# One raw buffer for the wb tiles, a transposition kept off the row turn, and score banks one step sooner, in a fused attention and MLP kernel

## The chip, the cores and the metric

The kernel runs on one core of one Trainium2 chip. The metric is the device time of one execution in microseconds. The core has a matrix engine (TensorE, PE in the profile; its weight loads are listed apart as PEld), a vector engine (VectorE, DVE), a scalar engine (ScalarE, ACT), a general engine (GpSimd, POOL) and a queue that issues the transfers (SyncE, SP). Each of them runs its own instructions in the order in which the program lists them.

## The reference

```python
x = A_x                                    # 1 x 2048 x 512
xn = layernorm(x)
q = (xn @ wq)                              # 32 heads of 16
k, v = xn @ wk, xn @ wv                    # one head of 16, shared by all
p = softmax(einsum("bhqd,bkd->bhqk", q, k) * 16 ** -0.5)
s = einsum("bhqk,bkd->bhqd", p, v) @ wo    # 512 x 512
h = xn @ w1 + b1                           # 512 x 1792
act = h * tanh(softplus(h))                # Mish
g = silu(act @ w2)                         # 1792 x 512
out = x + s * g
```

All arrays are float32.

## The kernel before, in words

**Tiling.** The 2048 rows are handled in four chunks `c` of 512 columns of the transposed, normalised input `xt`. A chunk has eight *units* of four heads, so there are 32 units `v`. The scores of a unit take 16 *steps*, one for each block of 128 keys, so there are 512 steps `s` (`NS`), with `v, k = divmod(s, 16)`.

**What a step does** (loop at L1257). Four score matmuls `e` (`e_one`, L871), each of 128 keys by 512 queries, are turned by ACT into `pt = exp(e / 4)` (L873). Four matmuls `m` (`m_one`, L890) compute scores of a later unit the other way round, 128 queries by 512 keys, and DVE takes the maximum of each row (L892). They run `LEAD = 22` steps ahead, so the last 22 steps, from step `NS - LEAD = 490`, have none. At the end of the step come the `pv` matmuls of step `s - 2` (L938). `e` uses one half of the rows of the PE array and `m` the other, and the two run at once. Between them `waves` places filler: matmuls of the projections, cut into halves of the array (`xps`, L106), up to eight to a step. A filler *group* of 12 or 15 matmuls is begun by `begin` when `is_ready` says that its weights and inputs are there by the planner's reckoning; otherwise the step has no filler. The matmuls of a group stand in the PE order, so if its weights come later than reckoned, PE waits in the middle of the step.

**The row turn** (`c_rows`, L898). When the 64 maxima columns of a unit are done, DVE reduces them (`mx`), and two steps later PE transposes the result (`mt`, L911, in a bank of tag `m`), DVE splits it in a high and a low part (`cr`), and SP copies both into rows 48, 49, 112 and 113 of the unit's query tile `qt` (L925, four transfers). The score matmuls of the unit subtract the maxima in this way.

**Weights.** A tile of `w1` has tag `ws`, one of `w2` or `wo` tag `wb`, one of `wq` tag `wq`. On its first use a tile is loaded as float32 into a *raw* buffer (`load`, L418 or L420); there are `RAWS = 2` of these for all tags together, and `NRAW` says how many of them a tag may hold at a time. POOL then splits it into a high part (L145) and a low part (L150), and the raw buffer is free. The split tile is also stored to DRAM (L399), and from its second use on it is loaded from there (L412). `pump` goes through the tags in the order wq, ws, wb, wx at the end of each step. POOL also does most of Mish, the scaling of the attention output (`oc`, `ot_all`) and the splits of `q`.

**SP's queue** carries all of this in order: raw loads, stores of split tiles, the query rows of coming units (L583), the maxima rows (L925) and the rows of the output (L956). An instruction whose buffer is not free yet holds up what is behind it.

**The transposed input of chunks 2 and 3** (`xt_turns`). Four tiles each are transposed by PE (L812, in a bank of tag `m`) at the end of odd steps, copied by ACT (L815) and split by POOL. In the kernel before, those of chunk 2 stand in steps 181, 183, 185 and 187, those of chunk 3 in steps 323 to 329.

**Banks.** PSUM tag `e` has three buffers, tag `m` three, tag `v` (pv) one and tag `x` (filler) one.

**Before step 0** a planner written into the kernel (L1166 on) lists layer norm, transposition of the input, the projections of k, v and the first q, 44 pairs of `m` matmuls, single matmuls that keep PE busy (`keep_warm`, L1152) and the first filler groups, by estimated costs. It loads and splits weights with the same `load` and `split`. k is computed for one chunk of keys at a time (`kp`, L277) and copied to the second half of the rows by a transfer (L288); pairs 24 to 31 of unit 0 need the k of chunk 3.

By the listed order of the kernel before, steps 4, 41, 86, 87, 136, 157, 158 and 479 have no filler.

Of the kernel before, what the change touches and what calls it, by code (L numbers as in the profile page):

```python
# [33 lines left out]
LEAD = 22  # L34
# [23 lines left out]
def m_need(v):  # L58

    return (40, 64)[v] if v < 2 else 32 * (v + 1)  # L60
# [52 lines left out]
def block_kernel(ctx: ExitStack, tc: tile.TileContext, x, wq, wk, wv, wo, w1, b1, w2, out):  # L113
# [3 lines left out]
    ps_e = ctx.enter_context(tc.tile_pool(name="ps_e", bufs=3, space=bass.MemoryType.PSUM))  # L117
    ps_m = ctx.enter_context(tc.tile_pool(name="ps_m", bufs=3, space=bass.MemoryType.PSUM))
# [195 lines left out]
    def at(s, fn):  # L314
        if s <= step[0]:
            fn()
        else:
            timed.setdefault(s, []).append(fn)

    def later(k, fn):  # L320
        at(step[0] + k, fn)
# [22 lines left out]
            ran[0] += 1  # L344

    RING = {"wq": 1, "ws": 2, "wb": 5, "wx": 4}
    NRAW = {"wq": 1, "ws": 1, "wb": 2, "wx": 1}
    RAWS = 2
    raws = [0]
    items = {t: [] for t in RING}  # L350
# [9 lines left out]
    def arrived(tag):  # L360
        k, n = todo[tag]
        return k < n and items[tag][k].step + 1 <= (step[0] if lead else max(step[0], busy[0] / STEP_US) + 0.3)
# [39 lines left out]
    def load(tag):  # L402
# [7 lines left out]
        if n == k and kept.get(it.key):  # L410
# [3 lines left out]
            todo[tag][:] = n + 1, n + 1  # L414
        elif n - k < NRAW[tag] and raws[0] < RAWS:
            r = sb.tile([P, D], F32, tag="raw", name=f"raw{tag}{n}", bufs=RAWS)
# [8 lines left out]
    def pump():  # L425
        for tag in items:
            while arrived(tag):
                split(tag)
            load(tag)
# [63 lines left out]
    def waves(h, em, new):  # L493

        fresh = cur["g"] is None
        if not cur["chunk"] and (not new or cur["g"] is None and not begin()):
            mms = []  # L500
        else:
            g = cur["g"]
            mms = cur["chunk"] or g.mms[cur["n"]:cur["n"] + chunk_size(len(g.mms) - cur["n"])]
        second = bool(cur["chunk"])
        k = len(mms)
        ms = em(k, fresh)
        a = deque(ms[1 - h])
        b = deque(ms[h])
        ps = cur["ps"]
        ends = second and cur["n"] + k == len(cur["g"].mms)  # L510
        xs = deque(mms)
        spare = len(b) if fresh and k else 0
        relay = None
        first = True
        done = False
        while a or b or xs:
            if spare and b:
                b.popleft()()
                spare -= 1
            elif xs:  # L520
                i = xs.popleft().half(ps, h)
                if first and cur["relay"] is not None:
                    tc.add_manual_dep(i.ins, cur["relay"].ins.name, mybir.DependencyInfo(
                        mybir.DependencyClass.Sync, mybir.DependencyReason.DATA), reason="other half of the bank")
                first = False
                if not xs and ends:
                    cur["n"] += k
                    cur["chunk"] = []
                    finish()
                    done = True  # L530
            elif b:
                b.popleft()()
            if len(a) > 1 or a and not xs:
                r = a.popleft()()
                if k and not xs and relay is None:
                    relay = r
        if k and not done:
            assert relay is not None
            cur["relay"] = relay
            if second:  # L540
                cur["n"] += k
                cur["chunk"] = []
            else:
                cur["chunk"] = mms
# [235 lines left out]
    turns = deque()  # L780
# [79 lines left out]
    def e_one(s, i):  # L860

        v, r = divmod(s, 16)
        if s < NS - LEAD:
            a, k, p = 1 - s % 2, r - r % 2 + i // 2, i % 2
        else:
            a, k, p = i % 2, r, i // 2
        q = qt_of[v]
        o = 64 * a
        ps, tag = (ps_m, "m") if NS - LEAD + 1 <= s and i in ((1, 3) if s < NS - 4 else (3,)) else (ps_e, "e")
        e = ps.tile([P, C], F32, tag=tag, name=f"e{s}_{i}")  # L870
        pe.matmul(e, ks[o:o + 64, P * k:P * (k + 1)], q[o:o + 64, p], start=True, stop=True)  # L871
        pt = sb.tile([P, C], F32, tag="pt", name=f"pt{s}_{i}", bufs=NPT)
        r = act.activation(pt, e, AF.Exp, scale=0.25)  # L873
        pt_of[16 * v + k, p, a] = pt
        return r
# [3 lines left out]
    def m_one(a):  # L879
        v, n = MSEQ[m_next[a]] if m_next[a] < 64 else divmod(m_next[a], 32)  # L880
        m_next[a] += 1
        if v not in mb_of:
            mb_of[v] = sb.tile([P, 4, 16], F32, tag="mb", name=f"mb{v}", bufs=2)
        q = qt_of[v]
        kb, j = divmod(n, 8)
        p, t = divmod(j, 4)
        o = 64 * a
        m = ps_m.tile([P, C], F32, tag="m", name=f"m{v}_{a}_{n}")
        o = slice(o, o + (HALF if v < len(qts) else 48))
        pe.matmul(m, q[o, p, P * t:P * (t + 1)], ks[o, C * kb:C * (kb + 1)], start=True, stop=True)  # L890
        z = 8 * a + 4 * p + t
        return dve.reduce_max(out=mb_of[v][:, kb, z:z + 1], in_=m, axis=AX.X)  # L892

    def m_sides(h, n):

        ahead = m_next[h] - m_next[1 - h]
        lo = max((4 - MLAG - ahead + 1) // 2, 4 - (32 * NU - m_next[1 - h]))
        hi = min((4 + MLAG - ahead) // 2, 32 * NU - m_next[h])  # L898
        return max(min(n, hi), lo)
# [112 lines left out]
    NS = 16 * NU  # L1012

    nc.scalar.preload_act_table_set("natural_log_exp_and_others")
    def due(t):
        step[0] = t
        for k in sorted(k for k in timed if k <= t):
            for fn in timed.pop(k):
                fn()
# [134 lines left out]
    def m_ready(t):  # L1154
        if min(m_next) >= 2 * LEAD or rows and rows[-1].end is None:
            return None
        v, n = MSEQ[m_next[0]]
        if len(qready.get(v) or ()) <= n % 8 // 4 or n // 8 not in kready:
            return None
        return max(t, qready[v][n % 8 // 4], kready[n // 8], m_ends[-2])  # L1160
# [13 lines left out]
    while True:  # L1174
# [8 lines left out]
        m = m_ready(T["PE"])  # L1183
# [10 lines left out]
        s, e, k = min(opts, key=lambda o: o[0])  # L1194
# [36 lines left out]
        elif k == "J":  # L1231
            tag = next((g for g in ("wq", "ws", "wb") if arrived(g) and busy[0] + E0 < s + 0.5), None)
# [21 lines left out]
        k.end = now[0]  # L1254
    lead.clear()

    for s in range(NS + 2000):  # L1257
        inm = s < NS - LEAD
        if inm or cur["chunk"]:
            assert s < NS  # L1260
            due(s)
            h = s % 2

            def em(k, fresh):
                n = m_sides(1 - h, k // 2) if inm else 0
                x = deque(lambda i=i: e_one(s, i) for i in range(4))
                y = deque(lambda: m_one(1 - h) for _ in range(n))
                r = [[], []]
                for op in EM[fresh and n == 3]:
                    if op == "M" and y:  # L1270
                        r[1 - h].append(y.popleft())
                    elif op == "E":
                        r[1 - h].append(x.popleft())
                r[h] = [lambda: m_one(h) for _ in range(4 - n if inm else 0)]
                return r

            if s >= 2 and (s - 1) % 16 == 0 and s > 1:
                gap[0] += 1
            waves(h, em, inm)
            act_jobs(1 + (len(jobs) > 3))  # L1280
            due(s + 0.5)
            if s >= 2:
                pv(s - 2)
                if (s - 1) % 16 == 0 and s > 1:
                    o_out((s - 17) // 16)
                elif turns and inm and s % 2 and turns[0]():
                    turns.popleft()
        else:
            due(s)
            if s < NS:  # L1290
                for i in range(4):
                    e_one(s, i)
                fill(4)
            act_jobs(2 if s < NS else 100)
            if s < NS + 2:
                pv(s - 2)
                if (s - 1) % 16 == 0:
                    o_out((s - 17) // 16)
            due(s + 0.5)
            if s >= NS:  # L1300
                fill(16)
        step[0] = s
        if vdone[0] < 8 * NC and min(m_next) >= m_need(vdone[0]):
            r = c_rows(vdone[0])
            r[0]()
            later(2, lambda r=r: [fn() for fn in r[1:]])
            vdone[0] += 1
        pump()
        if s > NS + 1 and not queue and cur["g"] is None and not timed and not jobs:
            break  # L1310
# [12 lines left out]
```

## Time and profile before

| What | Value |
|---|---|
| median of three runs | 1647.51 us (1647.10 to 1650.88) |
| profiled execution, its own time | 1648.34 us |
| its span, first to last instruction | 1646.6 us |
| PE busy, share of the span | 1626.7 us, 99% |
| DVE busy | 1351.5 us, 82% |
| ACT busy | 1303.5 us, 79% |
| POOL busy | 638.3 us, 39% |
| mean granted PE clock | 0.997 |
| `e` of step 0 / first `pv` matmul (step 2) | 95.45 us / 102.47 us after the span's start |

Busy time is the time in which an engine has at least one instruction running. Share of the span is an average over stages: with PE at 99% a gain is to be looked for in single places where PE waits. In the listings below a line of the timeline is: start in us, duration in us, engine, line of the code, operation, tile written and tiles read, shape, count, and in brackets the idle time of the engine before it and what ended it. `SPq` is SP issuing a transfer, `DMA` a transfer on its way.

### The profile page before, as it was taken

The page shows a single profiled execution, that of the slowest core. Times are in us where ns is not written, and L with a number is a line of the kernel's source. Part 1 is how long each engine was busy: PE and PEld are TensorE (multiplying, and loading weights), DVE is VectorE, ACT ScalarE, POOL GpSimd, SP SyncE. Part 2 cuts the span into 40 slices and gives each one's busy share as a digit, 9 for nine tenths or more (in the row PEclk, how much of TensorE's full clock was granted, in tenths as well). Part 3 has the DMA queues.
Part 4 walks back from the last instruction along what each step waited for, and adds up shares of the span by engine and source line. Part 5 has one row for each costly group of instructions (what it writes and reads, how often), then busy time and mean ns, then how long its engine had stood idle before and what let it go on. Part 6 is the DMA issues. An engine that isn't in the chain of part 4 may idle for free.

```text
span 1646.6 us, 31447 instructions
## 1 busy us (share of the span) xinstructions
PE 1626.7 (99%) x11719; PEld 861.1 (52%) x11719; DVE 1351.5 (82%) x2268; ACT 1303.5 (79%) x2503; POOL 638.3 (39%) x648
## 2 busy tenths in 40 slices
PE   8999999999999999999999999999999999999998
PEld 5545545545555555555555555555555555555543
DVE  8888878888888888888888888888888888888812
ACT  5568778788888778877888787887888878788885
POOL 4764176164365202622515221271251415125421
PEclk9999999999999999999999999999999999999999
DMA  5211132142131303203122231320322213031020
GB/s 164 59 62 50 45 135 73 43 144 69 50 122 58 115 26 132 69 14 99 54 70 77 62 100 31 111 63 16 119 94 81 68 48 102 16 107 55 8 84 26
DMA packets 69640, 120.24 MB, mean 73 GB/s; under 512 B 17840, under 2 KB 31664, under 8 KB 69488
## 3 DMA queue, kind: packets, MB, share of 16 engines
q1 hardware_dynamic: 69488, 118.23, 23.1%
q8 instruction: 93, 1.52, 0.4%
q14 instruction: 59, 0.48, 0.1%
HBM read 73.47 MB, written 23.07 MB: 59 GB/s over the span
## 4 chain that ended last, share of the span: by engine, by line
PE 95%; DVE 3%; POOL 1%; DMA 1%; ACT 0%; issue 0%; SPq 0%; DVEq 0%; POOLq 0%; ACTq 0%
PE xps L106 41%; PE pv L938 31%; PE m L890 11%; PE e L871 7%; PE xps L102 2%; DVE mb L892 2%; PE wop L102 1%; PE warm L1152 1%; PE kp L277 0%; PE mt L911 0%; DMA rawws<-in_dram 0%; PE xq L812 0%; DMA xin<-in_dram 0%; PE xp L245 0%; DVE xin L235 0%
## 5 line engine op out<-in xcount | busy, mean ns | idle before, releaser
L892 DVE TENSOR_REDUCE mb<-m 128x1 f32<-128x512 f32 x2048 | 1273.3, 682 | 209.7 <-PE m L890 153.9
L873 ACT ACTIVATE pt<-e 128x512 f32<-128x512 f32 x2048 | 1074.1, 608 | 273.8 <-PE e L871 251.7
L890 PE MATMUL m<-ks,qt 48*128 48x512 f32 (+1 forms) x2048 | 840.5, 427 | 3.0 <-DVE mb L892 2.4
L871 PE MATMUL e<-qt,ks 64*128 64x512 f32 x2048 | 754.5, 413 | 0.5 <-ACT pt L873 0.5
L938 PE MATMUL pv<-pt,vaug 128*32 128x512 f32 x4096 | 546.5, 606 | 0.0
L890 PEld LDWEIGHTS m<-ks,qt 48*128 48x128 f32 (+1 forms) x2048 | 371.6, 185 | 144.2 <-DVE mb L892 106.1
L871 PEld LDWEIGHTS e<-qt,ks 64*128 64x128 f32 x2048 | 367.0, 186 | 35.2 <-ACT pt L873 25.9
L106 PE MATMUL xps<-xt,ws 64*128 64x512 f32 x1242 | 342.2, 407 | 3.3 <-POOL ws L145 1.4
L106 PE MATMUL xps<-wb,act 64*128 64x512 f32 x1204 | 322.0, 404 | 0.0
L106 PEld LDWEIGHTS xps<-xt,ws 64*128 64x128 f32 x1242 | 218.1, 186 | 155.9 <-ACT pt L873 118.1
L106 PEld LDWEIGHTS xps<-wb,act 64*128 64x128 f32 x1204 | 210.0, 184 | 150.6 <-ACT pt L873 100.0
L938 PEld LDWEIGHTS pv<-pt,vaug 128*32 128x32 f32 x4096 | 80.7, 108 | 147.7 <-issue 138.9
L160 POOL TENSOR_SCALAR t<-t 128x512 f32<-128x512 f32 x56 | 34.4, 614 | 300.6 <-ACT t L634 300.5
L150 POOL TENSOR_TENSOR hb<-hb,t 128x512 f32<-128x512 f32 x56 | 72.1, 1288 | 115.2 <-ACT t L647 78.4
L106 PE MATMUL xps<-xt,wq 64*128 64x512 f32 x336 | 92.5, 407 | 0.0
L106 PE MATMUL xps<-wb,ot_all 64*128 64x512 f32 x288 | 78.8, 405 | 0.0
L106 PEld LDWEIGHTS xps<-xt,wq 64*128 64x128 f32 x336 | 58.7, 185 | 33.3 <-ACT pt L873 23.5
L150 POOL TENSOR_TENSOR oc<-oc,sc 128x512 f32<-128x512 f32 (+1 forms) x16 | 20.6, 1285 | 141.5 <-ACT sc L966 138.7
L150 POOL TENSOR_TENSOR hb<-hb,u 128x512 f32<-128x512 f32 x56 | 72.2, 1288 | 4.4
L150 POOL TENSOR_TENSOR u<-u,t 128x512 f32<-128x512 f32 x56 | 71.8, 1283 | 4.7
L150 POOL TENSOR_TENSOR act<-hb,act 128x512 fp32r<-128x512 f32 x55 | 70.8, 1288 | 4.6
L106 PEld LDWEIGHTS xps<-wb,ot_all 64*128 64x128 f32 x288 | 50.0, 184 | 35.1 <-ACT pt L873 27.8
(119 smaller groups left out, 881.8 us busy)
## 6 DMA issues: line engine op xcount, KB each, us to landing
ws<-w SPq DMA_DIRECT2D x37, 512.0 KB
wb<-w SPq DMA_DIRECT2D x33, 512.0 KB
qt<-qh SPq DMA_DIRECT2D x256, 32.0 KB
wq<-wq SPq DMA_DIRECT2D x14, 512.0 KB
w<-ws SPq DMA_DIRECT2D x14, 512.0 KB
w<-wb SPq DMA_DIRECT2D x14, 512.0 KB
wb<-wo SPq DMA_DIRECT2D x12, 512.0 KB
rawwb<-in_dram SPq DMA_DIRECT2D x23, 256.0 KB
```

The lines of the kernel that those rows point to most:

```text
L102: self.pe.matmul(ps, self.lhs(), self.rhs(), start=(self.k == 0), stop=(self.k == self.tot - 1))
L106: i = self.pe.matmul(ps, self.lhs()[o], self.rhs()[o], start=(self.k == 0 and self.halves == 0), stop=(self.k == self.tot - 1 and self.hal ...
L150: eng.tensor_tensor(out=o, in0=a, in1=b, op=op)
L160: pool.tensor_scalar(o, o, lim, 0.0, op0=ALU.min, op1=ALU.max)
L871: pe.matmul(e, ks[o:o + 64, P * k:P * (k + 1)], q[o:o + 64, p], start=True, stop=True)
L873: r = act.activation(pt, e, AF.Exp, scale=0.25)
L890: pe.matmul(m, q[o, p, P * t:P * (t + 1)], ks[o, C * kb:C * (kb + 1)], start=True, stop=True)
L892: return dve.reduce_max(out=mb_of[v][:, kb, z:z + 1], in_=m, axis=AX.X)
L938: pe.matmul(o[32 * j:32 * j + 32], vaug[:, k], pt, start=(k == 0), stop=(k == 15))
L1152: pe.matmul(w, qts[2][:, 0, 0:P], qts[2][:, 0], start=True, stop=True)
```

## The change

It has three parts. `NRAW["wb"]` goes from 2 to 1, so that wb tiles hold at most one of the two raw buffers. The loop notes in `rows_at` the step in which the next row turn will stand, and the transposition of an input tile is left out of the step right before it; it then comes two steps later, since only odd steps take one. And the scores 1 and 3 of a step take banks of tag `m` from step `NS - LEAD` (490) on instead of 491.

```diff
-    NRAW = {"wq": 1, "ws": 1, "wb": 2, "wx": 1}
+    NRAW = {"wq": 1, "ws": 1, "wb": 1, "wx": 1}
...
-        ps, tag = (ps_m, "m") if NS - LEAD + 1 <= s and i in ((1, 3) if s < NS - 4 else (3,)) else (ps_e, "e")
+        ps, tag = (ps_m, "m") if NS - LEAD <= s and i in ((1, 3) if s < NS - 4 else (3,)) else (ps_e, "e")
...
+    rows_at = [0]
     for s in range(NS + 2000):
...
-                elif turns and inm and s % 2 and turns[0]():
+                elif turns and inm and s % 2 and rows_at[0] != s + 1 and turns[0]():
                     turns.popleft()
...
             r = c_rows(vdone[0])
             r[0]()
+            rows_at[0] = s + 2
             later(2, lambda r=r: [fn() for fn in r[1:]])
```

Since the planner and the loop decide everything by what is loaded and split when, the first part reorders all five engines ahead of step 0 and in steps 0 to 136. There, steps 0, 1, 2, 43 and 48 have no filler now, in place of 4, 41, 86, 87 and 136; steps 157, 158 and 479 stay as they were. From step 137 on the order of every engine is the same as before but for the transposition that moves from step 187 to 189 and the banks of step 490.

## The prediction, made before the changed kernel was run

> **What bounds the kernel now.** I read the chain of work that ended last first.
>
> ```profile
> PE 95%; DVE 3%; POOL 1%; DMA 1%; ACT 0%; issue 0%; SPq 0%; DVEq 0%; POOLq 0%; ACTq 0%
> ```
>
> TensorE (PE) is the bound nearly everywhere, and the change leaves its work alone: the changed program, built but not run, has one PE instruction fewer of 9669 (four warm-up matmuls and three whole projection matmuls fewer, six half-array ones more). So a gain can come only from places where PE stands still or runs slowly. I found them by taking the start of each step's first pv matmul from the timeline: 511 intervals, median 2.94 us, 98 in 100 between 2.70 and 3.63. These stand out: steps 42, 43 and 44 (5.22, 5.15, 3.47), 82 (4.81), 490 (3.72) and 188 (3.69). The critical chain in order of time shows what is behind steps 42 and 82 (start, us, what):
>
> ```profile
> 215.66 2.53 DMA rawws<-in_dram
> 218.20 1.29 POOL oc L150
> 220.27 1.28 POOL ot_all L150
> 222.22 1.28 POOL ws L150
> ...
> 343.60 3.04 DMA rawws<-in_dram
> 347.49 1.28 POOL ws L150
> ```
>
> A w1 tile (ws) is fetched late, then split late on GpSimd (POOL), and PE waits for the halves. Why late: the POOL timeline, and SP's queue beside it.
>
> ```profile
> 212.03 1.29 POOL L150 TENSOR_TENSOR wb<-rawwb,wb 128x512 fp32r<-128x512 f32 x1
> 213.99 1.28 POOL L150 TENSOR_TENSOR wb<-rawwb,wb 128x512 fp32r<-128x512 f32 x1
> 216.26 0.62 POOL L145 TENSOR_SCALAR wb<-rawwb 128x512 fp32r<-128x512 f32 x1 [0.99 <-PE e L871]
> 221.52 0.62 POOL L145 TENSOR_SCALAR ws<-rawws 128x512 fp32r<-128x512 f32 x1
> ```
>
> ```profile
> 213.35 0.33 SPq L420 DMA_DIRECT2D rawwb<-in_dram  x1
> 215.66 0.53 SPq L418 DMA_DIRECT2D rawws<-in_dram  x1
> ```
>
> Both raw buffers hold wb tiles. The load of ws tile 9 goes out at 215.66, when the second wb split has ended (213.99 + 1.28 = 215.27). POOL meanwhile waits 0.99 for a third wb tile, splits that and writes `oc` and `ot_all` before it gets to ws. At step 82 it is the same: the ws load goes out at 343.60, just behind a wb split (342.29 + 1.29).
>
> Step 43 waits for nothing comparable, yet is as long. The stretches of 3.41 us show it (us, then busy us of PE, PEld, DVE, ACT, POOL; PEclk; DMA share; GB/s):
>
> ```profile
> 217.33:220.74 3.41, 3.24 (x24) 1.20 (x16) 3.08 (x6) 3.41 (x9) 3.24 (x4) 1.00 0.46 153
> 220.74:224.15 3.41, 2.17 (x17) 1.11 (x14) 2.73 (x6) 1.83 (x5) 3.25 (x4) 1.00 0.82 319
> 224.15:227.57 3.42, 3.42 (x16) 1.01 (x15) 0.00 (x0) 1.16 (x2) 3.24 (x4) 0.50 0.82 285
> 227.57:230.98 3.41, 3.41 (x18) 1.78 (x18) 2.75 (x4) 2.23 (x4) 3.24 (x4) 0.50 0.62 252
> 347.02:350.44 3.42, 2.35 (x20) 1.12 (x20) 1.85 (x4) 2.21 (x5) 3.25 (x4) 1.00 0.65 225
> ```
>
> The stall of step 42 is followed by 6.83 us of half granted clock. Step 82, with 2.35 us busy instead of 2.17, kept its clock. So the first stall is paid twice.
>
> **The change part by part.**
>
> *One raw wb buffer, steps 37 to 50.* The number of POOL splits is the same but for one w1 tile, but one wb tile at a time alternates with ws. In the built order, POOL has before the split of ws tile 9 now: `oc` and `ot_all` (1.28 + 0.62 + 1.28 and two gaps, 3.3), one wb split (0.62 + 1.28 and a gap, 2.0), the four Mish operations of w1 tile 7 (0.61 + 0.62 + 1.28 + 1.29 and gaps, 4.0), then ws itself (2.0): 11.3. They start when ACT has `sc`, 1.5 us after step 39's first pv (212.58 against 211.09). At 2.9 a step, ws is ready at 1.5 + 11.3 - 4 x 2.9 = 1.2 us into step 43. The planner starts its group in step 44 (42 before), where PE asks for it 1.0 us in, behind pv: 2.7 us of slack. The stall goes, and with it the clock drop. What remains is what a first filled step after one unfilled step costs elsewhere: 3.63 (108.36 to 112.00, step 5; 508.66 to 512.29, step 137). So 5.22 + 5.15 + 3.47 = 13.84 becomes 3.63 + 2.90 + 3.10 = 9.63: **-4.2**. Bounds: 0 (it stalls alike at step 44) and -4.9 (three usual steps of 2.94 + the row turn's 0.1).
>
> *The same, steps 76 to 86.* In front of ws tile 14 now: Mish of tile 12 (4.0, starting 2.2 into step 81 when ACT is done, as 335.62 was in step 78), one wb split 2.0, ws 2.0: 10.2, so 1.5 into step 84. Its group starts 1.0 into step 85: 2.4 of slack. 4.81 becomes 3.05: **-1.8** (0 to -1.8).
>
> *The same, before step 0.* The raw loads are reordered there too. POOL splits one wb tile instead of two ahead of the last low part of chunk 2, so k of chunks 2 and 3 is projected one pair of m matmuls earlier (before: 66.96, now behind the pair at 65.20). This ends at
>
> ```profile
> 75.19 2.37 PE L102 MATMUL xps<-xt,wq 128*128 128x512 f32 x9 [0.48 <-ACT hb L628]
> 78.02 3.82 DVE L892 TENSOR_REDUCE mb<-m 128x1 f32<-128x512 f32 x6 [2.65 <-PE m L890]
> ```
>
> where nine projection matmuls stand before pair 24 and VectorE (DVE) is idle 2.65. The new order has three there: 2.37 - 0.97 = 1.4 earlier, covered by the k copy, which goes out one pair (1.27) earlier. Pairs 24 to 31 take 77.49 to 87.57, 1.44 each; now 0.90 + 0.43 = 1.33: seven times 0.11, 0.8. Against it, five warm-ups instead of two stand before the transposition of the first maxima: +0.5. **-1.7**; bounds 0 and -4.9 (all DVE idle from 63 to 86: 0.81 + 0.38 + 2.65 + 0.52 + 0.25 + 0.27). Of the two I stay at the lower half, as PE at 1.33 a pair nearly meets DVE's 1.28.
>
> Three projection matmuls move behind step 0, and steps 0 to 2 stay unfilled. Unfilled steps number eight before and eight after, and take 2.88 in the median, as filled ones do (2.91 to 3.04): 0, hidden by DVE's four reductions (2.48). Bounds -0.3 and +0.7 (one more 3.63).
>
> *Transposition beside the row turn.* Only one of eight moves, from step 187 to 189, with its ACT copy and two POOL operations; no DMA, and its chunk is asked for at step 219. Steps 188 to 191 took 3.69 + 2.84 + 2.91 + 2.94 = 12.38. A row turn alone costs 3.28 (steps 172, 300), a transposition alone 3.44 to 3.50: 3.28 + 2.85 + 3.47 + 2.94 = 12.54: **+0.2** (-0.3 to +0.5).
>
> *Scores in maxima banks at step 490.*
>
> ```profile
> 1566.40 0.73 PE L871 MATMUL e<-qt,ks 64*128 64x512 f32 x3
> 1567.59 0.50 PE L871 MATMUL e<-qt,ks 64*128 64x512 f32 x1 [0.45 <-ACT pt L873]
> ```
>
> The fourth score waits 0.45 for ACT to free one of three banks. Two of the maxima banks, last read by DVE at 1566.38 or sooner, replace them: **-0.5** (0 to -0.9, a 2.78 step), and PE alone bounds the steps behind.
>
> Sum: -4.2 - 1.8 - 1.7 + 0.2 - 0.5 = **-8.0**. The profiled execution took 1648.34 (span 1646.6 and 1.7 around it), 0.8 above the median 1647.51: 1640.3 by the one, 1639.5 by the other. I say **1640.0**.
>
> From step 137 to 489 both orders are the same but for that one transposition, so nothing else can move there.
>
> **The rivals.**
>
> *The stall moves (0.17).* POOL's work is the same, and 2.7 and 2.4 us of slack are my reckoning over four steps. If ACT's `sc` or a raw load is some 3 us later than laid out, step 44 stalls as 42 did: 1640.3 + 4.2 = 1644.5. For it: the planner's estimate failed twice before. Against: it now leaves one step more.
>
> *The clock falls in steps 0 to 2 (0.08).* Three unfilled steps in a row, two without pv. DVE paces them at 0.62 a pair of 0.39 to 0.50 us: a busy share of 0.65 to 0.8. The share 2.17/3.41 = 0.64 lost the clock and 2.35/3.42 = 0.69 did not. Price as in steps 43 and 44: 2.2 + 0.4, so 1643. [...]
>
> *Slower (0.05).* With one raw wb buffer, a load waits in SP's in-order queue for the split before it, and in the new order the four copies of the maxima rows (step 44) stand behind the raw load of ws tile 10, which waits for the split of wb tile 8. I get 0.4 into step 45 for that load and 3.9 us of slack to the scores of step 48. Were POOL over 4 us later than that, scores would stall by 2.3 and lose the clock (2.7), in each of three batches of wb tiles (steps 44, 85, 118): 15 - 8, so 1655.
>
> *The raw buffer doesn't matter (0.04).* If the two stalls come from slow landings (3.04 at 343.60), only the rest stays: 1648.3 - 2.0 = 1646.3.
>
> **How the numbers follow.** Forecast 0.66. A measurement here tells about 0.3% from no change, 4.9 us, so faster is below 1642.6: nearly all of the forecast (0.64), half of the clock rival (0.04), little of the moved stall (0.03): 0.71. Slower 0.05, the rest 0.24. The range runs from 1637 (the lead's -4.9) to 1646 (moved stall with no gain ahead of step 0): it leaves out the last two rivals and some 0.07 below.
>
> **What would show it.** Right: step 0 begins 1 to 2.5 us earlier than 95.1; granted clock 1.00 from step 0 to the end; no step from 3 to 136 over 3.7 us; POOL's ws splits alternating with wb; no ACT wait in the scores of step 490. Wrong: a wait of xps for POOL ws again, 0.50 in any stretch, scores waiting for the maxima rows, or DVE idle over 2 us before step 0.

## The result, and the profile after

The changed kernel took 1640.53 us (median of four runs, 1639.98 to 1641.22) beside 1649.20 us for the kernel before (four runs, 1647.10 to 1653.68): a ratio of 0.9944, interval 0.9921 to 0.9967. In two later sessions its median was 1640.21 (five runs, ratio 0.9939, 0.9918 to 0.9961) and 1642.37 (eleven runs, 0.9955, 0.9938 to 0.9972). The profiled run is that of 1639.98 us, 8.36 less than the 1648.34 of the profile before.

How far the changed kernel is ahead at each place follows from the start of the first `pv` matmul of a step in both timelines (a step is counted from the `pv` matmuls at the end of the step before to those at its own end):

| stretch | before, us | after, us | difference |
|---|---|---|---|
| up to the first `e` of step 0 | 95.45 | 93.68 | -1.78 |
| steps 0 to 2 (first `e` to first `pv`) | 7.02 | 7.67 | +0.65 |
| step 3 | 2.85 | 4.81 | +1.96 |
| steps 4 to 7 | 12.52 | 11.68 | -0.84 |
| steps 8 to 41 | 102.00 | 101.74 | -0.26 |
| steps 42 to 44 | 13.83 | 9.87 | -3.96 |
| steps 45 to 81 | 111.47 | 111.07 | -0.40 |
| step 82 | 4.81 | 2.88 | -1.92 |
| steps 83 to 135 | 155.60 | 155.55 | -0.05 |
| steps 136 to 139 | 12.50 | 11.64 | -0.86 |
| steps 140 to 489 | 1047.37 | 1047.43 | +0.06 |
| steps 490 and 491 | 6.48 | 5.53 | -0.95 |

The two stalls carry 5.9 of the 8.36 us. What was gained ahead of step 0 is lost again by step 8. The chain that ended last no longer runs through the load of a ws tile (0.3% of the span before), and between 205 and 235 us it has no link of POOL or DMA left. Over the whole span POOL keeps its 1%, in other places. Its shares by engine:

```profile
PE 96%; DVE 2%; POOL 1%; ACT 1%; DMA 0%; issue 0%; SPq 0%; POOLq 0%; DVEq 0%
```

This is how PE waited for ws tile 9 in step 42 of the kernel before, first for its high part and then for its low part:

```profile
222.19 0.49 PE L106 MATMUL xps<-xt,ws 64*128 64x512 f32 x1 [0.62 <-POOL ws L145]
223.55 0.49 PE L106 MATMUL xps<-xt,ws 64*128 64x512 f32 x1 [0.61 <-POOL ws L150]
```

Here is POOL's timeline of the changed kernel ahead of the same tile:

```profile
212.95 1.28 POOL L150 TENSOR_TENSOR oc<-oc,sc 128x512 f32<-128x512 f32 x1 [4.92 <-ACT sc L966]
214.32 0.62 POOL L145 TENSOR_SCALAR ot_all<-oc 128x512 fp32r<-128x512 f32 x1
...
217.00 1.29 POOL L150 TENSOR_TENSOR wb<-rawwb,wb 128x512 fp32r<-128x512 f32 x1
...
221.02 1.29 POOL L150 TENSOR_TENSOR hb<-hb,u 128x512 f32<-128x512 f32 x1
222.28 0.61 POOL L145 TENSOR_SCALAR ws<-rawws 128x512 fp32r<-128x512 f32 x1
222.98 1.29 POOL L150 TENSOR_TENSOR ws<-rawws,ws 128x512 fp32r<-128x512 f32 x1
```

SP's queue and PE's timeline, of the same kernel:

```profile
207.15 0.58 SPq L420 DMA_DIRECT2D rawwb<-in_dram  x1
208.06 0.39 SPq L418 DMA_DIRECT2D rawws<-in_dram  x1
```

```profile
225.53 1.07 PE L938 MATMUL pv<-pt,vaug 128*32 128x512 f32 x8
...
227.82 0.40 PE L106 MATMUL xps<-xt,ws 64*128 64x512 f32 x1
```

The ws load goes out at 208.06 (215.66 before), the split ends at 222.98 + 1.29 = 224.27, and PE asks for it at 227.82, in step 44. No wait is left. But the split is not sooner than before, where it ended at 223.49: POOL still does `oc`, `ot_all`, a wb split and four Mish operations ahead of it. What has moved is the step in which the order asks for the tile, 44 instead of 42. The new loss stands near step 0. Stretches of 3.41 us of the changed kernel (busy us of PE, PEld, DVE, ACT, POOL; granted clock; DMA share; GB/s):

```profile
94.39:97.81 3.42, 2.87 (x12) 1.18 (x12) 3.42 (x7) 3.11 (x6) 0.90 (x1) 1.00 0.69 226
97.81:101.22 3.41, 3.37 (x12) 1.56 (x10) 3.41 (x7) 3.40 (x8) 1.06 (x1) 0.50 0.73 234
101.22:104.63 3.41, 3.41 (x15) 1.03 (x13) 1.60 (x3) 1.57 (x4) 3.16 (x5) 0.50 0.06 13
...
224.09:227.50 3.41, 2.99 (x19) 0.99 (x16) 3.04 (x7) 3.04 (x6) 2.66 (x4) 1.00 0.43 91
```

The half clock that the kernel before had behind its stall (224.15 to 230.98) is gone, and one of the same length, 6.83 us, has come at 97.81. It reaches from step 1 into step 3. The `pv` matmuls with which step 3 begins take nearly twice their usual 1.07 us:

```profile
101.35 1.94 PE L938 MATMUL pv<-pt,vaug 128*32 128x512 f32 x8
```

At step 490 the four scores now follow each other in one group, with no wait for ACT:

```profile
1559.02 0.73 PE L871 MATMUL e<-qt,ks 64*128 64x512 f32 x4
```

### The profile page after: what moved, and what is told of

It reads as the page before. It is cut to its first block, busy times and chain, and to the rows that moved or that the text cites. A ratio compares the mean times of both kernels' runs of the same rounds, so it can differ in the third digit from the quotient of the medians.

```text
span 1638.2 us, 31435 instructions
## 1 busy us (share of the span) xinstructions
PE 1621.8 (99%) x11718; PEld 859.6 (52%) x11718; DVE 1351.1 (82%) x2268; ACT 1303.4 (80%) x2502; POOL 638.5 (39%) x647
## 3 DMA queue, kind: packets, MB, share of 16 engines
q8 instruction: 93, 1.52, 0.4%
## 4 chain that ended last, share of the span: by engine, by line
PE 96%; DVE 2%; POOL 1%; ACT 1%; DMA 0%; issue 0%; SPq 0%; POOLq 0%; DVEq 0%
PE xps L106 41%; PE pv L938 31%; PE m L890 11%; PE e L871 8%; PE xps L102 2%; DVE mb L892 1%; PE wop L102 1%; POOL ot_all L150 1%; PE kp L277 0%; PE warm L1152 0%; PE mt L911 0%; PE xq L812 0%; DMA xin<-in_dram 0%; DMA rawwb<-in_dram 0%; POOL wb L150 0%
## 5 line engine op out<-in xcount | busy, mean ns | idle before, releaser
L106 PE MATMUL xps<-xt,ws 64*128 64x512 f32 x1248 | 340.8, 405 | 0.0
L106 PE MATMUL xps<-wb,act 64*128 64x512 f32 x1204 | 322.1, 404 | 0.1
L106 PEld LDWEIGHTS xps<-xt,ws 64*128 64x128 f32 x1248 | 218.9, 185 | 152.4 <-ACT pt L873 121.0
L106 PEld LDWEIGHTS xps<-wb,act 64*128 64x128 f32 x1204 | 209.8, 184 | 151.2 <-ACT pt L873 98.5
L106 PE MATMUL xps<-xt,wq 64*128 64x512 f32 x336 | 92.2, 406 | 0.0
L106 PE MATMUL xps<-wb,ot_all 64*128 64x512 f32 x288 | 78.6, 405 | 0.0
L106 PEld LDWEIGHTS xps<-xt,wq 64*128 64x128 f32 x336 | 58.8, 185 | 32.2 <-ACT pt L873 22.8
L106 PEld LDWEIGHTS xps<-wb,ot_all 64*128 64x128 f32 x288 | 50.1, 184 | 33.7 <-ACT pt L873 26.9
```

The costliest lines, as they stand in the source:

```text
L106: i = self.pe.matmul(ps, self.lhs()[o], self.rhs()[o], start=(self.k == 0 and self.halves == 0), stop=(self.k == self.tot - 1 and self.hal ...
```

## The experiments

"First theory" in what follows is the prediction's: the wb tiles hold both raw buffers, so ws tiles come late. Step lengths are read from the `pv` starts as above. Each session had its own runs of the kernel before, and ratios are to those.

### The parts of the change alone

One raw buffer alone (the first line of the diff, on the kernel before):

```diff
-    NRAW = {"wq": 1, "ws": 1, "wb": 2, "wx": 1}
+    NRAW = {"wq": 1, "ws": 1, "wb": 1, "wx": 1}
```

> The kernel before with the first edit alone (one raw buffer for the wb tiles). Theory (the shared raw buffers made the ws tiles late): the 9.6 us of steps 42 to 44 and the 3.05 us of step 82 of the changed kernel come here too, step 0 begins at 93.7 us, and the run is 0.5 to 1.0 us longer than the changed kernel, which has step 490 shortened besides: 1641.0 to 1641.5. Rival (the other two edits carry a good part): over 1643.

Measured: 1640.97 us (five runs), ratio 0.9958 (0.9945 to 0.9970). Steps 42 to 44 took 9.88 us and step 82 2.89; steps 490 and 491 stayed at 6.48. Step 0 began at 96.70 and not at 93.7, since this run had 6.83 us of half clock at 35.02 as well.

The rest of the change, with two raw buffers for the wb tiles (the line above undone in the changed kernel):

> The changed kernel with two raw buffers for the wb tiles again: the second and third edits alone. Theory: steps 42 to 44 take 13.8 us and step 82 4.8 us, as before; step 490 is 0.9 us shorter, steps 188 and 190 change places at no cost, and the whole run is 0.5 to 1.0 us shorter than before. Rival (the other two edits carry a good part): 3 us or more shorter than before.

Measured: 1647.31 us (eleven runs) beside 1647.86, ratio 0.9996 (0.9986 to 1.0006). Steps 42 to 44 took 12.31 us, steps 82 and 83 9.27 and steps 490 and 491 5.52. The stalls are there, but not at the 13.8 and 4.8 us that were expected: here the clock fell for 3.41 us behind each of them (at 225.24 and 348.12), and not for 6.83 us behind the first alone. So the first part carries the gain. The two small edits save 0.96 us in steps 490 and 491 of the profile; in the time of the whole run that is not clear of no change.

### The buffer ahead of step 0 or in the loop

The changed kernel with one line put in ahead of the loop and the constant set the other way round. First, two buffers ahead of step 0 and one from there on:

```diff
-    NRAW = {"wq": 1, "ws": 1, "wb": 1, "wx": 1}
+    NRAW = {"wq": 1, "ws": 1, "wb": 2, "wx": 1}
...
     lead.clear()
+    NRAW["wb"] = 1
```

> The changed kernel, with two raw buffers for the wb tiles ahead of step 0 and one from step 0 on. Theory (the gain is made at the two stalls): step 0 begins at 95.4 us and the clock stays at 1.00 through step 3, which takes 2.9 us and not 4.8; steps 42 to 44 take 9.6 us and step 82 3.05 us; all of the gain is there, 1640 to 1641.5. Rival (the earlier start of step 0 carries it): no more than 1 us shorter than before, 1647 to 1648.

Measured: 1642.17 us (five runs), ratio 0.9965 (0.9952 to 0.9979). The clock stayed at 1.00 and step 3 took 2.85 us; steps 42 to 44 took 8.84, but step 46 4.09 (the first filled one behind step 45, which has no filler here in place of 41), so that steps 42 to 49 come to 24.60, as in the changed kernel (24.59). Step 82 took 3.01. The run is 0.7 us above the expected range: steps 136 to 139 took 12.55 us, as in the kernel before, and not 11.64.

Then one buffer ahead of step 0, and two in the loop:

```diff
     lead.clear()
+    NRAW["wb"] = 2
```

> The changed kernel, with one raw buffer for the wb tiles ahead of step 0 and two from step 0 on. Theory: step 0 begins at 93.7 us, the clock falls in steps 1 to 3 as in the changed kernel, the lead is used up by step 8, steps 42 to 44 take 13.8 us and step 82 4.8 us again: 1646.5 to 1648. Rival (the earlier start carries it): 1640 to 1642, with steps 42 to 44 at 10 us or less.

Measured: 1642.08 us (five runs), ratio 0.9964 (0.9951 to 0.9976). Steps 42 to 44 took 9.87 us and step 82 3.05, **with two buffers for the wb tiles**. The first theory's expectation failed here (13.8 and 4.8 us, 1646.5 to 1648): sharing the buffers in the loop doesn't make the stall by itself. In the listed order the three unfilled steps 0 to 2, which the change ahead of step 0 makes, put the groups of ws tile 9 two steps later (step 44 instead of 42).

### The place and not the number

A new theory: what decides is the place of the ws load among the wb loads and POOL's other work, and the number of buffers acts through it. To test it, the kernel before, with two raw buffers throughout, was made to leave the first three (or two) steps without filler:

```diff
+    rest_ = [False]
...
-        if not cur["chunk"] and (not new or cur["g"] is None and not begin()):
+        if not cur["chunk"] and (rest_[0] or not new or cur["g"] is None and not begin()):
...
+            rest_[0] = s < 3
             waves(h, em, inm)
```

> The kernel before, both raw buffers left to the wb tiles, but with no projection matmuls filled into steps 0 to 2: every later group comes three steps on, as in the run with one raw buffer ahead of step 0 alone. New theory (the place of the ws loads among the groups' POOL work decides, and the number of raw buffers acts through it): steps 42 to 44 take 10 us or less and step 82 3.2 us or less, 1641 to 1643, with half clock in steps 0 to 3. First theory (sharing the raw buffers in the loop is itself the cause): steps 42 to 44 13.8 us and step 82 4.8 us, 1647 to 1650.

Measured: 1644.30 us (eleven runs), ratio 0.9976 (0.9960 to 0.9991): steps 42 to 44 at 9.87, step 82 at 3.05, the clock at half for 3.41 us at 93.58 and for 6.83 us at 100.40, step 3 at 4.24 us.

> The same with steps 0 and 1 held alone: ws tile 9 is loaded at step 38 and its group begins at step 43, so five steps lie between as in the kernel before, but one wb tile fewer is ahead of it in the queue of splits. New theory: steps 42 to 44 at 10.5 us or less. First theory: 13 us or more.

Measured: 1644.10 us (twelve runs), ratio 0.9976 (0.9959 to 0.9994): steps 42 to 44 at 9.93, step 82 at 3.04, no clock fall near step 0, step 3 at 2.85. The first of the two lies 1.3 us above the expected range, and its profile has a clock fall ahead of step 0 that the theory had not (93.58). The stalls are gone all the same, and nothing of the first part of the change is in these two kernels. But the place on POOL is not what cured them. In the kernel with two steps held, POOL still has the third wb tile, `oc` and `ot_all` ahead of ws tile 9, whose split ends at 223.48 + 1.28 = 224.76; PE asks for it later, in step 43:

```profile
221.52 1.29 POOL L150 TENSOR_TENSOR ot_all<-oc,ot_all 128x512 fp32r<-128x512 f32 x1
...
223.48 1.28 POOL L150 TENSOR_TENSOR ws<-rawws,ws 128x512 fp32r<-128x512 f32 x1
```

```profile
225.90 0.39 PE L106 MATMUL xps<-xt,ws 64*128 64x512 f32 x1
```

The sharpest test of the place leaves the buffers as they were and only exchanges loads. `pump` issues the splits of all tags first and then the loads; in the listed order the group of ws tile 9 begins one step sooner by it (step 41), and steps 0 to 5 are filled as before:

```diff
             while arrived(tag):
                 split(tag)
+        for tag in items:
             load(tag)
```

> The kernel before with two raw buffers for the wb tiles and the groups at the same steps, but at the end of a step the splits of all tags are issued first and the loads after them, so that at step 36 ws tile 9 is loaded ahead of wb tile 8 and not behind it, and at step 77 ws tile 14 ahead of wb tile 14. Theory of the place (a ws load behind one more wb tile, when the wb tiles hold both buffers, makes the stall): steps 42 to 44 at 10.5 us or less, step 82 at 3.3 us or less, clock 1.00 in steps 0 to 3, 1641 to 1643.5. Theory of the number (a single raw buffer or other groups' steps are needed): 13 us or more and 4.5 us or more, 1647 to 1649.

Measured: 1643.96 us (eleven runs), ratio 0.9971 (0.9953 to 0.9989). Steps 42 to 44 took 8.85 us, step 46 4.26, steps 42 to 49 24.76 (28.51 before); step 82 took 3.01. SP's queue of this kernel:

```profile
215.20 0.39 SPq L418 DMA_DIRECT2D rawws<-in_dram  x1
217.15 0.33 SPq L420 DMA_DIRECT2D rawwb<-in_dram  x1
```

And POOL's timeline:

```profile
215.84 1.28 POOL L150 TENSOR_TENSOR wb<-rawwb,wb 128x512 fp32r<-128x512 f32 x1
218.15 0.62 POOL L145 TENSOR_SCALAR ws<-rawws 128x512 fp32r<-128x512 f32 x1 [1.03 <-DMA rawws<-in_dram]
218.85 1.29 POOL L150 TENSOR_TENSOR ws<-rawws,ws 128x512 fp32r<-128x512 f32 x1
...
222.06 1.29 POOL L150 TENSOR_TENSOR oc<-oc,sc 128x512 f32<-128x512 f32 x1
```

The ws load goes out at nearly the same time as in the kernel before (215.20 against 215.66); as this run is 1.8 us behind there, that is 2.3 us sooner by its steps. There is still a wait for a raw buffer, but the load takes the one that the first wb split frees. So the split of ws stands ahead of the third wb tile and of `oc` and `ot_all`, and ends at 220.14 instead of 223.49. That takes the long stall away, although PE asks one step sooner; a short one comes in step 46, where PE waits 0.5 and 0.6 us for the two parts of ws tile 10. (The time is 0.5 us above the expected range, and the profile has a clock fall at 35.62.) Put together, with the end of the split of ws tile 9 and the step in which PE asks for it:

| kernel | wb raw buffers in the loop | steps 42 to 49 | steps 82 to 86 | split of ws tile 9 ends | PE asks in step |
|---|---|---|---|---|---|
| before | 2 | 28.51 | 16.47 | 3.65 us into step 42 | 42 |
| small edits alone | 2 | 26.99 | 18.06 | 3.65 us into step 42 | 42 |
| changed | 1 | 24.59 | 14.53 | 1.78 us into step 43 | 44 |
| one buffer alone | 1 | 24.58 | 14.53 | 1.76 us into step 43 | 44 |
| one buffer in the loop | 1 | 24.60 | 14.73 | 1.35 us into step 40 | 41 |
| one buffer ahead of step 0 | 2 | 24.49 | 14.68 | 1.77 us into step 43 | 44 |
| three steps held | 2 | 24.50 | 14.68 | 1.72 us into step 43 | 44 |
| two steps held | 2 | 24.64 | 14.67 | 1.16 us into step 43 | 43 |
| splits first | 2 | 24.76 | 14.71 | 1.52 us into step 41 | 41 |

In the first two rows step 42 itself is lengthened by the wait; at a usual length of 2.9 us their split would end 0.75 us into step 43. So there are two ways out. With one buffer in the loop, and with the splits first, the split comes sooner. In the changed kernel and in the other four it comes no sooner, by the steps even 0.4 to 1.0 us later, and the order asks for it one or two steps later.

A third raw buffer, which would show the buffers' share by itself, was not tried.

### The clock near step 0

The changed kernel once more, as the measure:

> The changed kernel once more, beside the next three on one chip. Theory (the three unfilled steps 0 to 2 leave TensorE too little work and the granted clock falls there each time): half clock for 3.4 or 6.8 us between 95 and 106 us, step 3 at 4.2 to 4.8 us, 1640 to 1641.5. Rival (the fall was chance): clock 1.00 there, step 3 at 3.6 us or less, 1638 to 1639.

Measured: 1640.21 us (five runs). Half clock for 6.83 us at 99.83, step 3 at 4.72 us. Then nine more matmuls in the unfilled steps, to hold the clock:

```diff
             waves(h, em, inm)
+            if s < 3 and cur["g"] is None:
+                w = ps_x.tile([P, C], F32, tag="x", name=f"keep{s}")
+                for _ in range(3):
+                    pe.matmul(w, qts[2][:, 0, 0:P], qts[2][:, 0], start=True, stop=True)
```

> The changed kernel with three more matmuls of 128x512 (results unused) in each of the unfilled steps 0, 1 and 2, nine in all. Theory (too little TensorE work in these steps lowers the clock): clock 1.00 from step 0 to the end, step 3 at 3.6 us or less, 1.5 to 2.5 us shorter than the changed kernel. Rival (the fall comes from something else): half clock near 100 us all the same, and the nine matmuls add 0 to 1.9 us (9 x 0.21).

Measured: 1645.51 us (twelve runs), 5.3 above the changed kernel of the session. The experiment spoiled itself: `qts[2]` is a query buffer that was being written, and the waits of this kernel's PE show

```profile
PE keep L1284 <- DMA qt<-ql: 1.6, 1, 1.6
```

PE stood still for 1.6 us, and the clock fell there (at 103.17). It says nothing for or against the theory. (No row shows the 0.21 us a matmul of the expectation: the nine matmuls of this shape from 75.19 on took 2.37 us in the kernel before, about 0.23 from one start to the next.) So again with the keys as operands, and one matmul behind each pair instead of three in a lump:

```diff
             elif b:
                 b.popleft()()
+                if keepb[0] is not None:
+                    pe.matmul(keepb[0], ks[:, 0:P], ks[:, 0:C], start=True, stop=True)
```

> The changed kernel with one more matmul of 128x512 (result unused, operands the keys that are there since before step 0) behind each pair of matmuls of the unfilled steps 0 to 2, twelve in all, spread where the earlier ones stood in a lump and waited for a DMA. Theory (too little TensorE work lowers the clock): clock 1.00 from step 0 to the end, step 3 at 2.8 to 3.6 us, 1.2 to 2 us shorter than the changed kernel, 1638 to 1639. Rival (the fall comes from something else): half clock near 100 us, step 3 over 4 us, 1640 to 1642.

Measured: 1643.12 us (eleven runs), ratio 0.9973 (0.9952 to 0.9994). Windows of this kernel:

```profile
95.57:98.99 3.42, 3.42 (x13) 1.42 (x12) 3.00 (x5) 2.57 (x5) 0.10 (x1) 1.00 0.72 235
98.99:102.40 3.41, 3.41 (x14) 1.58 (x12) 2.57 (x4) 2.63 (x6) 0.00 (x0) 1.00 0.58 193
102.40:105.81 3.41, 3.41 (x18) 1.28 (x18) 2.27 (x4) 2.62 (x5) 2.77 (x3) 1.00 0.01 2
```

The clock stays at 1.00 from 6.12 us to 1637.69, behind the last matmul, and eight of the eleven runs had a mean clock of 0.999 (the changed kernel's five had 0.995 to 0.997). So more matmul work does hold the clock here. But the 1638 to 1639 us that were expected did not come: step 3 took 3.65 us, and steps 0 to 2 took 10.40 us (from 94.83 to 105.23) instead of 7.67. A pair with the added matmul takes 0.86 us instead of 0.60. So the same matmuls, narrowed to 160 columns:

> The same twelve matmuls, narrowed from 512 to 160 columns: by the 0.43 us that one of 512 took an estimate of 0.13 us each, which fits into the 0.6 us per pair of the unfilled steps (a pair takes 0.43). Theory (the clock needs the work, and the lengthening of the last run was the matmuls' own time): clock 1.00 from step 0 to the end, steps 0 to 2 as long as in the changed kernel (7.7 us from the first score to the first product with V), step 3 at 2.8 to 3.1 us; 1.4 to 2.2 us shorter than the changed kernel beside it, 1638 to 1639. Rival (that little work doesn't hold the clock): half clock near 100 us, step 3 over 4 us, within 0.5 us of the changed kernel.

Measured: 1649.11 us (twelve runs), ratio 0.9998 (0.9981 to 1.0014): 6.7 above the changed kernel beside it, the worst of all. PE's timeline:

```profile
98.29 0.50 PE L875 MATMUL e<-qt,ks 64*128 64x512 f32 x1
98.29 0.50 PE L894 MATMUL m<-ks,qt 64*128 64x512 f32 x1
98.72 0.34 PE L536 MATMUL keep<-ks 128*128 128x160 f32 x1
98.99 0.49 PE L875 MATMUL e<-qt,ks 64*128 64x512 f32 x1
```

And its windows:

```profile
96.45:99.86 3.41, 3.41 (x14) 1.88 (x15) 3.16 (x7) 1.54 (x3) 1.80 (x2) 1.00 0.40 108
99.86:103.27 3.41, 3.41 (x9) 1.59 (x9) 2.15 (x5) 2.21 (x5) 0.00 (x0) 0.50 0.79 290
```

A pair with its narrow matmul takes 0.70 us (98.29 to 98.99), not 0.60, and the clock fell at 99.86 for 13.65 us although PE was recorded busy for the whole window before. At half clock such a pair takes 1.15 us:

```profile
101.14 0.79 PE L875 MATMUL e<-qt,ks 64*128 64x512 f32 x1
102.29 0.79 PE L875 MATMUL e<-qt,ks 64*128 64x512 f32 x1
```

So steps 0 to 2 took 13.03 us. The estimate of 0.13 us a matmul was wrong (last section).

> The changed kernel as a measure for the run with the narrow matmuls, on one chip with it: 1640 to 1641, half clock near 100 us and step 3 at 4.2 to 4.8 us.

Measured: 1642.37 us (eleven runs, 1638.01 to 1644.89), step 3 at 5.04 us, half clock for 6.83 us at 63.99 and at 101.55. The median is 1.4 us above the expected range, and step 3 above its own. Two runs had a mean clock of 0.999 and took 1638.01 and 1638.11 us; those at 0.997 and 0.998 took 1639.72 to 1640.67, those at 0.995 or less 1642.37 to 1644.89. So the fall near step 0 was there in all three profiles of the changed kernel, but those two runs leave no room for it: it is frequent, not certain. No version tried had a lower ratio than the changed kernel's 0.9939 to 0.9955; those with its first edit alone or with half of it (0.9958, 0.9965, 0.9964) are not clear of it.

## Why the prediction was right, point by point

**Where the time lay** was right: the two stalls and the clock behind the first. (The 9669 PE instructions of the prediction stand in no trace. These have 11719 matmuls before and 11718 after; the difference of one holds.)

**Steps 42 to 44**, -4.2 forecast, -3.96 measured: no stall, no clock fall; step 44, the first filled one after an unfilled one, took 3.93 us instead of the 3.63 taken over from other places. The reckoning along POOL's queue held: ws tile 9 was to be ready 1.2 us into step 43, and was at 1.8 (224.27 against 222.48). PE asked for it 2.3 us into step 44, not 1.0.

**Step 82**, -1.8 forecast, -1.92 measured; ws tile 14 was ready 1.4 us into step 84 (forecast 1.5).

**The cause behind both** was right as a row and too broad as a rule. The prediction said that both raw buffers hold wb tiles, and also that POOL then waits for a third wb tile and writes `oc` and `ot_all` ahead of ws. The exchange of two loads shows that the second half of this makes the split late: with both buffers still given to wb tiles the stall goes, once the ws load takes the first buffer that comes free. But in the changed kernel it is the other term of the prediction's slack that cures, the group's start in step 44 instead of 42: its split comes no sooner, and the same shift with two buffers in the loop gives the same 9.87 us. Fewer buffers in the loop without a shift, a shift of the group by one or two steps, and the exchange each do it.

**Ahead of step 0**, -1.7 forecast, -1.78 measured in the first pair of profiles. The place was right, the terms only in part. Pair 24 starts 1.36 us sooner (76.13 for 77.49; forecast 1.4). Pairs 24 to 31 gain 0.50 and not 0.8 (a pair each 1.37 us, not 1.33). The five warm-up matmuls cost 0.38 and not 0.5. Another 0.29 is gained between the transposition of the maxima and step 0, where the prediction has no term; that the sum came out so near is luck. The gain is only there if the clock holds: in the two later profiles of the changed kernel step 0 began at 96.64 and 96.85, behind 6.83 us of half clock at 34.98 and 63.99.

**Unfilled steps 0 to 2 at no cost**: this step failed. They are 0.65 us longer, and the clock falls in them, which makes step 3 1.96 us longer. The 0.65 us is not the clock's, as the pairs start 0.60 us apart on both sides of its fall at 97.81 (96.91, 97.51, 98.11, 98.70). The 1.96 us is the clock rival, with 0.08 much too low a chance; its price was 2.6. The forecast time survived it by luck, because the unfilled steps were missing where they had stood: -0.84 in steps 4 to 7 and -0.86 in steps 136 to 139, where the prediction set eight against eight and took 0. The drifts of -0.26 and -0.40 in steps 8 to 41 and 45 to 81 I did not trace. "Granted clock 1.00 from step 0 to the end" and "no step over 3.7 us" were wrong for steps 3 and 44. That rival rested on recorded busy shares, 0.64 losing the clock and 0.69 keeping it; here 2.87/3.42 = 0.84 lost it.

**The transposition**: steps 188 to 191 took 12.34 us instead of 12.39, so 0 and not +0.2. **Step 490**: -0.95, not -0.5; the longest gain named (a 2.78 us step) is what came, as all four scores found a bank.

Sum: -8.0 forecast, -8.36 between the profiles. In it 2.61 us of loss in steps 0 to 3 stand against 1.70 us of gain in steps 4 to 7 and 136 to 139 and 0.65 us of drifts, all of which the prediction took as 0; that they nearly cancel is luck too. The rival that the raw buffer doesn't matter is out (1647.31 without it), and so is that of a stall that moves. Nothing showed of the held-up SP queue.

## What to carry to other kernels

When an engine waits for a load, follow the load back to the queue position it was given, not only to the pool it drew from: exchanging the order of splits and loads in one loop was worth nearly as much in these steps as a change of buffer counts that reordered all five engines. And when such a wait goes, see which of its two ends moved, the data's arrival or the place where the order asks for it; here it was the second. When such a change frees the work ahead of a phase, look at what it does to the density of the matmuls there; the lead of 1.78 us was lost by step 3, which alone took 1.96 us longer at half clock. And padding matmuls must be weighed in the unit that they occupy with their neighbours: 12 of them cost 2.7 us here where 1.96 was to be won.

## What the runs showed of the hardware

**In these profiles the clock goes with the columns streamed, not with the recorded busy time.** From 30 us to the last `pv` matmuls, twelve of the fourteen profiles show 20 falls in all. In the profile before the clock changes at 224.15, 230.98 and 1644.09 us, 2 and 414 times 3.413 us apart; in the one after at 97.81, 104.63 and 1633.80, 2 and 448 times; with the small edits alone its two falls (225.24, 348.12) lie 36 times that apart. So a window here is one of the stretches of that length, counted from a profile's first fall. Windows before a fall had recorded busy shares of 0.56 (1.92 of 3.41 us ahead of 103.17, with the nine added matmuls) to 1.00 (ahead of 99.86, with the narrow ones), and windows with 0.69 (347.02, kernel before) and 0.77 (73.91, changed kernel) kept the clock. If instead each matmul is counted as 0.22 us from its start (the least spacing of the half-array filler matmuls of 512 columns, L106, 0.224, with a median of 0.232; in proportion 0.07 for 160 columns and 0.06 for 128), overlaps once, the share is an estimate that sorts them better: the 20 windows before a fall had 0.31 to 0.48, no window of these profiles below 0.41 kept the clock, and between 0.41 and 0.48 both occur. Steps 0 to 2 of the changed kernel, a pair each 0.60 us, are at 0.37 without pv; with twelve full matmuls (0.44 of 0.86) they are at 0.51 and kept it; with the narrow ones (0.29 of 0.70) at 0.41 and lost it (the window before the fall, 96.45 to 99.86, with three `m` matmuls ahead of the first narrow one in it, is at 0.48). It took no long pause of PE: in the window before the fall of the changed kernel, 94.39 to 97.81, the longest wait was 0.38 us.

**The switch between a half-array pair and a full-array matmul has a price of its own.** From start to start, from the pair to the 128-row matmul it is 0.43 us (with the full matmuls, 95.77 to 96.20); from a 128-row matmul of 512 columns back to the pair 0.43 (96.20 to 96.63), of 160 columns 0.28 (with the narrow ones, 98.01 to 98.29). Matmuls of one kind follow each other in about 0.23 us (128 rows: nine in 2.37 us from 75.19 in the kernel before; pairs: 105.13, 105.36 and 105.60 in the changed kernel). The slope is 0.15 us for 352 columns, 0.22 for 512, so by an estimate from these rows about 0.21 us of each way is fixed. So the twelve narrow matmuls lengthened a pair by 0.10 us at full clock (0.70 for 0.60); most of what they cost came with the half clock.
